# A half chunk of batch 0's queries loaded later, with buffers of its own, in a fused linear-attention and gated-MLP kernel

## The chip, the core and the metric

The kernel runs on one core of one Trainium2 chip. The metric is the device time of one execution in microseconds (us); for the kernel before, the median of 3 runs is 248.44 us (248.17 to 248.79). Times inside an execution are counted from its first instruction. TensorE is PE in the profile's rows (PEld is its weight load), VectorE is DVE, ScalarE is ACT, GpSimd is POOL, SyncE is SP.

## What is computed

Eight batches of eight heads, 576 positions and 64 columns go through a linear attention, and its result through a gated MLP. The reference, cut to what matters:

```python
theta = pi / 2 * pos / 576
phi(x) = concat([relu(x) * cos(theta), relu(x) * sin(theta)])   # 64 -> 128 columns
q_p, k_p = phi(q), phi(k)
kv  = einsum('bhsf,bhsd->bhfd', k_p, v)
z   = k_p.sum(over s)
out = (q_p @ kv) / (q_p @ z + 1e-6)      # per head; heads side by side: x, 4608 x 512
h   = ((x @ w1) * (x @ w2)) @ w3         # 512 -> 1024 -> 1024
y   = h @ w_out                          # 1024 -> 512, float32
```

## The kernel before

**Tiles.** A batch's 576 positions are five chunks: 0 to 3 of 128 rows and chunk 4, a half one, of 64. For each batch the queries, keys and values are loaded from DRAM by GpSimd's DMA queue and cast to bfloat16 on the way. Features (`features`, lines 487 to 499) are made chunk by chunk: the cosine half on VectorE (line 491), the sine half on ScalarE for the first `n` heads (line 495) and on VectorE for the rest (line 498). Values are copied into a buffer `va` that has a column of ones (`prep_v`, line 510), so that one product gives `kv` and `z`. `kv` (lines 534 to 544) takes 40 small matmuls (line 539), in the order of the chunks 4, 0, 1, 2, 3 for odd batches, and brings the sums from PSUM to `kvs`: heads 0 to 3 by ScalarE (543), then heads 4 to 7 by VectorE (544). A query chunk is transposed on TensorE and copied out of PSUM (`q_tr`, lines 553 to 563) or, in later batches, transposed by a DMA of SyncE's queue. `num` (565 to 573) multiplies it with `kvs` in 8 matmuls into a pair of PSUM banks `pnum`; `norm` (575 to 586) divides by the last column in three VectorE instructions (582, 583, 584). The quotient is transposed to `xT` (`x_tr`, 606 to 612; later by DMA, `x_dma`).

**The MLP.** Nine tiles of 512 rows of `x` go through `ffn_groups` (649 to 724): products with `w1` and `w2` (line 655), their elementwise product (681, 698), and the product with `w34 = w3 @ w_out` (703), all through a ring of four PSUM banks `ffnps` that `ffn_tile` hands out. `w34` is built once in the kernel (`w34_mm`, line 470): eight products of 8 matmuls on blocks of `w3` that VectorE has transposed (`w3_tr`, line 460, ring of 3 buffers), each evicted by ScalarE (line 473).

**What sets the order.** Every engine works in order, and the order is written out in the string `PLAN` (lines 26 to 259). In it `f t` is the next piece of MLP tile t (four matmuls of 512 columns mostly), `w j l n` a piece of the `w34` product, `t3 j` a transpose of `w3`, `l b q 0` a load (first 64 partitions; `1` is the second 64), `lg` and `lt` loads behind a gate on GpSimd, `q04` the load of batch 0's chunk 4 (line 419), `q b c n`, `k b c n` and `v b c E` the features and the value copy on engine E (G is GpSimd, V VectorE, A ScalarE), `qt b c E` a query transpose and its copy, `kv`, `n`, `d` and `xt` (or `xd` and `qd` by DMA) as above. An entry's place sets only the order on each engine's queue; whoever is free goes ahead.

**Around the change.** Batch 0's first 512 rows open the kernel. Its chunk 4 is needed only for the second MLP tile (`f 1`), so it is loaded with batch 1, while `w34` is built. The feature buffer `qp` is one for all batches: chunk 4 of batch 0 must have been transposed before batch 1's chunk 4 is written. `kv 1` needs all of batch 1's keys and values. GpSimd's DMA issues pass through eight semaphores in turn, so each issue waits for the landing of the eighth before it.

Of the kernel before, what the change touches and what calls it, by code (L numbers as in the profile page):

```python
# [106 lines left out]
f 2
f 2; d 3 4; k 4 2; q 4 1 0
f 2; xd 2 3; xd 3 0; k 4 1; k 4 0; xd 3 4; qd 4 3; n 3 2
f 2; n 3 3; l 5 v 0  # L110
f 2
f 2; q 4 2; d 3 2
f 2
f 2
f 2; qd 4 0
f 3; l 5 v 1; k 4 4
# [41 lines left out]
f 4; xd 4 4; xd 5 0; lt 7 v 0
# [1 line left out]
f 4; q 6 4  # L160
f 4; k 6 0 2; q 6 2; n 5 3; k 6 1 6; xd 5 4; q 6 0 4
f 4
# [10 lines left out]
f 5; kv 6; sg; k 7 3 6; lt 7 q 1; qd 6 2
f 5; n 5 2; k 7 2; k 7 1; k 7 0 4; lg 7 v 1; qd 6 0
f 5; qd 6 4; xd 5 3; qd 6 3
f 5
f 5; d 5 2; xd 5 1; xd 5 2
f 5
f 5; n 6 0; d 6 0; v 7 2 A; q 6 1 4; v 7 0 V
f 5; q 7 2; q 7 0  # L180
f 5; xd 6 0
# [130 lines left out]
def kernel(  # L312
# [128 lines left out]
    nc.vector.memset(oneb[:], 1.0)
# [42 lines left out]
                      "qpT": qpT_bufs[b % 2], "x": {}, "n": {}}  # L484
        return att[b]

    def features(dst, rows, c, at, n=H, cos=True, sin=True):

        R = ROWS[c]
        if cos:  # L490
            nc.vector.tensor_scalar(out=dst[:R, c, :, 0:D], in0=rows[:R], scalar1=0.0,  # L491
                                    scalar2=cosv[:R, at:at + 1], op0=ALU.max, op1=ALU.mult)
        if sin:
            if n > 0:
                nc.scalar.activation(out=dst[:R, c, 0:n, D:F], in_=rows[:R, 0:n], func=ACTF.Relu,  # L495
                                     scale=sinv[:R, at:at + 1], bias=0.0)
            if n < H:
                nc.vector.tensor_scalar(out=dst[:R, c, n:H, D:F], in0=rows[:R, n:H], scalar1=0.0,
                                        scalar2=sinv[:R, at:at + 1], op0=ALU.max, op1=ALU.mult)
# [52 lines left out]

    def q_tr(b, c, on):
        R = ROWS[c]
        pst = ps_tr.tile([P, 8, 128], BF16, name="pst")
        for h in range(H):
            nc.tensor.transpose(pst[:, h, :], att[b]["qp"][:, c, h, :], identb[:])
        cols = ds(columns_of(b, c), R)
        if on == "both":
            nc.scalar.copy(out=att[b]["qpT"][:, 0:4, cols], in_=pst[:, 0:4, 0:R])  # L560
            nc.vector.tensor_copy(out=att[b]["qpT"][:, 4:8, cols], in_=pst[:, 4:8, 0:R])
        else:
            on(out=att[b]["qpT"][:, :, cols], in_=pst[:, :, 0:R])

    def num(b, c, tile=None, heads=range(H)):
        rows = out_rows(b, c)
        at = columns_of(b, c) - rows.start
        qpT, kvs = att[b]["qpT"], att[b]["kvs"]
        nt = tile or pnum()
        for h in heads:  # L570
            nc.tensor.matmul(nt[:, h // 4, ds((h % 4) * 65, 65)], lhsT=qpT[:, h, ds(at, 128)],  # L571
                             rhs=kvs[:, h, :], start=True, stop=True)
        att[b]["n"][c] = nt

    def norm(b, c, g0=0, ng=2):
        rows, R = out_rows(b, c), ROWS[c]
# [5 lines left out]
        nc.vector.tensor_scalar_add(out=den[rows, 0:ng], in0=n4[:, :, :, 64], scalar1=1e-6)  # L582
# [1 line left out]
        nc.vector.tensor_tensor(out=xblk[rows, g0:g0 + ng], in0=n4[:, :, :, 0:D],  # L584
                                in1=den[rows, 0:ng].unsqueeze(3).to_broadcast([R, ng, 4, D]),
                                op=ALU.mult)
# [260 lines left out]
```

## Time and profile before

| what | us |
|---|---|
| median of 3 runs | 248.44 |
| the profiled execution's own time | 247.68 |
| its span, first to last instruction | 245.8 |
| TensorE busy | 238.9 |
| VectorE busy | 147.9 |
| ScalarE busy | 118.5 |
| GpSimd busy | 88.9 |

How to read it: the span is 1.88 us shorter than the execution's own time; what lies around it is the launch. Busy time is the sum of the instructions' own durations. A row of the timeline gives the start, the time from the first start to the last end of a merged run of like instructions, the engine, the line, the operation with its output and input, the count, and, in square brackets, how long the engine sat idle before it and on whom it waited. Matmuls are pipelined, so a row's duration runs past the start of the next row; the distance between two starts is what a row occupies. The granted TensorE clock was 1.00 throughout.

### The profile page before, as it was taken

The numbers are of one execution on the slowest core, as the hardware profiler recorded it, in microseconds if no ns is written. First come the engines' busy times: TensorE is split into PE (matmuls) and PEld (weight loads), VectorE is DVE, ScalarE is ACT, GpSimd is POOL, SyncE is SP. The second block draws the span as 40 slices with busy tenths as digits, with TensorE's granted clock in tenths as the row PEclk, the third lists the DMA queues.
The fourth block names the chain that finished last, engine by engine and source line by source line (L and its number), as shares of the span: only waits on it lengthen the run. The fifth ranks groups of instructions, "written<-read, shape, count | busy, mean of one in ns | idle before, by whom it ended". The sixth has DMA issues, their size and how long they took to land.

```text
span 245.8 us, 5011 instructions
## 1 busy us (share of the span) xinstructions
PE 238.9 (97%) x1891; PEld 129.9 (53%) x1891; DVE 147.9 (60%) x373; ACT 118.5 (48%) x210; POOL 88.9 (36%) x171
## 2 busy tenths in 40 slices
PE   8899999989999999999999999999999999999994
PEld 3589434567964545445544544454545454444442
DVE  6976558968888546925855576378458327403320
ACT  2834323767756734755466436558343333323321
POOL 8854887534403170006124023024001000497800
PEclk9999999999999999999999999999999999999999
DMA  7999999999999999879999999999337332489933
GB/s 198 195 196 199 195 177 191 199 199 168 165 163 167 182 135 195 129 138 153 193 138 148 168 144 159 234 148 185 75 61 148 96 75 44 68 267 338 302 119 128
DMA packets 84552, 40.44 MB, mean 165 GB/s; under 512 B 48048, under 2 KB 82096, under 8 KB 84528
## 3 DMA queue, kind: packets, MB, share of 16 engines
q0 software_dynamic: 38832, 27.27, 69.3%
q1 hardware_dynamic: 45696, 12.85, 32.6%
q8 instruction: 15, 0.25, 0.4%
q14 instruction: 9, 0.07, 0.1%
HBM read 38.80 MB, written 9.44 MB: 196 GB/s over the span
## 4 chain that ended last, share of the span: by engine, by line
PE 77%; DMA 9%; POOL 6%; DVE 4%; issue 1%; DVEq 0%; POOLq 0%
PE ffnps L655 45%; PE ffnps L703 24%; DMA early<-in_moe_w_out_dram 4%; PE pnum L571 4%; PE pnum L539 3%; POOL early L403 3%; DMA kf<-in_k_dram 3%; DMA q<-in_q_dram 2%; DVE w3T L460 1%; POOL w2b L776 1%; POOL early L409 1%; DVE kp L491 1%; POOL w1b L776 1%; PE ffnps L720 1%; DVE qp L491 1%
## 5 line engine op out<-in xcount | busy, mean ns | idle before, releaser
L698 DVE TENSOR_TENSOR abT<-asb,ffnps 128x512 bf16<-128x512 bf16 x64 | 43.7, 685 | 56.8 <-PE ffnps L655 56.4
L655 PE MATMUL ffnps<-xT,w1b 128*128 128x512 bf16 (+2 forms) x352 | 76.0, 340 | 0.0
L655 PE MATMUL ffnps<-xT,w2b 128*128 128x512 bf16 (+2 forms) x352 | 76.0, 340 | 0.0
L693 ACT CAST asb<-ffnps 128x512 bf16<-128x512 f32 x64 | 37.4, 584 | 58.6 <-PE ffnps L655 45.5
L703 PE MATMUL ffnps<-w34b,abT 128*128 128x512 bf16 x280 | 65.0, 379 | 0.0
L655 PEld LDWEIGHTS <-w1b 128*128 128x128 bf16 x352 | 31.7, 98 | 28.4
L655 PEld LDWEIGHTS <-w2b 128*128 128x128 bf16 x352 | 31.6, 98 | 28.0
L703 PEld LDWEIGHTS <-abT 128*128 128x128 bf16 x280 | 26.2, 98 | 28.9
L584 DVE TENSOR_TENSOR xblk<-pnum,den 128x512 bf16<-128x512 f32 (+1 forms) x39 | 26.9, 691 | 1.5 <-DVE den L583 0.2
L415 POOL COPY seen<-asb 128x1 bf16<-128x1 bf16 x13 | 2.6, 198 | 50.5 <-ACT asb L693 50.4
L495 ACT ACTIVATE kp<-kf,sinv 128x512 bf16<-128x512 bf16 (+4 forms) x33 | 20.7, 656 | 0.3 <-DMA kf<-in_k_dram 0.3
L495 ACT ACTIVATE qp<-qs,sinv 128x512 bf16<-128x512 bf16 (+6 forms) x30 | 18.3, 626 | 1.9 <-DMA qs<-in_q_dram 0.8
L571 PEld LDWEIGHTS <-qpT 128*128 128x128 bf16 x320 | 15.0, 98 | 7.2
L709 ACT COPY early<-ffnps 128x512 f32<-128x512 f32 x19 | 11.1, 585 | 15.4 <-PE ffnps L703 14.2
L571 PE MATMUL pnum<-kvs,qpT 128*128 128x65 bf16 x312 | 15.9, 194 | 0.0
L491 DVE TENSOR_SCALAR kp<-kf,cosv 128x512 bf16<-128x512 bf16 (+1 forms) x40 | 14.4, 379 | 2.1 <-DMA kf<-in_k_dram 2.1
L470 PE MATMUL ffnps<-early,w3T 128*128 128x512 bf16 x64 | 14.5, 379 | 0.5 <-DVE w3T L460 0.5
L415 POOL COPY seen<-xT 128x1 bf16<-128x1 bf16 x6 | 1.2, 193 | 36.6 <-DMA xT<-xblk 36.6
L510 POOL COPY va<-vs 128x512 bf16<-128x512 bf16 (+1 forms) x13 | 8.2, 639 | 13.7 <-DMA vs<-in_v_dram 13.7
L491 DVE TENSOR_SCALAR qp<-qs,cosv 128x512 bf16<-128x512 bf16 (+1 forms) x35 | 12.5, 368 | 0.0
L372 POOL DMA_DIRECT2D vs<-in_v_dram x16 | 10.7, 681 | 2.4 <-PE ffnps L470 1.1
L460 DVE STREAM_TRANSPOSE w3T<-early 128x1024 bf16<-128x1024 bf16 x8 | 9.7, 1231 | 2.5 <-DMA early<-in_moe_w_dram 2.5
(90 smaller groups left out, 225.5 us busy)
## 6 DMA issues: line engine op xcount, KB each, us to landing
kf<-in_k_dram POOLq DMA_DIRECT2D x7, 320.0 KB, 7.5
early<-in_moe_w_dram POOLq DMA_DIRECT2D x16, 128.0 KB, 5.3
out_dram<-osb POOLq DMA_DIRECT2D x8, 256.0 KB, 5.2
qs<-in_q_dram POOLq DMA_DIRECT2D x6, 320.0 KB, 6.6
vs<-in_v_dram POOLq DMA_DIRECT2D x6, 320.0 KB, 8.0
kf<-in_k_dram POOLq DMA_DIRECT2D x7, 256.0 KB, 8.2
qs<-in_q_dram POOLq DMA_DIRECT2D x6, 256.0 KB, 7.9
vs<-in_v_dram POOLq DMA_DIRECT2D x6, 256.0 KB, 9.3
```

The lines of the kernel that those rows point to most:

```text
L372: eng.dma_start(out=t[ts(half, 64), :, 0:j, :].rearrange("p h j d -> p h (j d)"), in_=rows[:, span, :].rearrange("h (p j) d -> p h (j d)", ...
L460: nc.vector.transpose(out=w3Ts[jp][:, l0:l0 + n, :].rearrange("p l (c i) -> p l c i", c=4), in_=w3b[:, jp, :].rearrange("p (c l j) -> p l ...
L470: nc.tensor.matmul(acc[:, :], lhsT=w3T[:, lc, :], rhs=woutb[:, lc, :], start=(lc == 0), stop=(lc == 7))
L491: nc.vector.tensor_scalar(out=dst[:R, c, :, 0:D], in0=rows[:R], scalar1=0.0, scalar2=cosv[:R, at:at + 1], op0=ALU.max, op1=ALU.mult)
L495: nc.scalar.activation(out=dst[:R, c, 0:n, D:F], in_=rows[:R, 0:n], func=ACTF.Relu, scale=sinv[:R, at:at + 1], bias=0.0)
L571: nc.tensor.matmul(nt[:, h // 4, ds((h % 4) * 65, 65)], lhsT=qpT[:, h, ds(at, 128)], rhs=kvs[:, h, :], start=True, stop=True)
L584: nc.vector.tensor_tensor(out=xblk[rows, g0:g0 + ng], in0=n4[:, :, :, 0:D], in1=den[rows, 0:ng].unsqueeze(3).to_broadcast([R, ng, 4, D]), ...
L655: nc.tensor.matmul(out, lhsT=w[:, kc, ts(jc, 128)], rhs=x[:, kc, tok], start=(kc == 0), stop=(kc == 3))
L693: nc.scalar.copy(out=asb[:], in_=aT[:, :])
L698: nc.vector.tensor_mul(out=abT[:, jc, :], in0=asb[:], in1=bT[:, :])
L703: nc.tensor.matmul(ops[:, :], lhsT=abT[:, jc, ts(ms, 128)], rhs=w34b[:, jc, :], start=(jc == 0), stop=(jc == 7))
L709: nc.scalar.copy(out=osb[:, ms % 2, :], in_=ops[:, :])
```

## The change

Four edits, made together with a new order in `PLAN` from the `w34` stage on.

1. The load `q04` moves from ahead of batch 1's loads to behind the last of them (`l 1 v 1`).
2. Its features go to a buffer of their own, `late`, laid over the first two heads of the raw queries of batch 0 (`q0f`), whose upper 64 rows are cleared with batch 1's value rows. Its features, transpose, numerator and quotient move from the middle of the `w34` stage to behind `kv 1`'s place on VectorE, TensorE and ScalarE.
3. Its numerator goes to two banks of the MLP's ring instead of the pair `pnum`, and is normalized in two halves.
4. Of batch 1's value copies, chunks 4, 0 and 1 on GpSimd and 3 and 2 on VectorE become chunk 0 on GpSimd, 1 on ScalarE, and 4, 2 and 3 on VectorE. GpSimd's one copy stands ahead of the load `l 2 v 1` in its queue.

The plan between, before and after, cut to the entries between the last loads of batch 1 and `f 1`:

```diff
-... w3 3 6 2; q04; l 1 q 0; l 1 q 1; l 1 k 0
+... w3 3 6 2; l 1 q 0; l 1 q 1; l 1 k 0
...
-f 0; xt 0 3 V; l 1 v 1
+f 0; xt 0 3 V; l 1 v 1; q04
...
-f 0
+f 0; v 1 0 G
...
-w 3 0 4
-w 3 4 4; t3 5; q 0 4 0; t3 6
+w 3 0 4; t3 5
+w 3 4 4; t3 6
 w 4 0 4
-w 4 4 4
-w 5 0 4; qt 0 4 V; t3 7; q 1 4 2; q 1 1; q 1 0 0
-w 5 4 4; n 0 4; q 1 3 0; d 0 4
+w 4 4 4; t3 7; q 1 4 2; q 1 2 0
+w 5 0 4
+w 5 4 4; q 1 1; q 1 0
 w 6 0 4
-w 6 4 4; q 1 2 4; k 1 4 0; k 1 0; l 2 v 1; v 1 4 G
-w 7 0 4; v 1 0 G; v 1 1 G; k 1 3 0; k 1 2
-w 7 4 4; k 1 1 0
-f 0; qt 1 4 A; qt 1 2 A; l 3 q 0; v 2 2 G; v 1 3 V
-f 0; qt 1 0 A; v 1 2 V; kv 1
-f 0; qt 1 1 A; n 1 4; d 1 4; k 2 4; k 2 2 2
+w 6 4 4; q 1 3 2; qt 1 4 A; v 1 4 V; k 1 4 4; qt 1 1 A; l 2 v 1
+w 7 0 4; k 1 0
+w 7 4 4; k 1 2 2; k 1 1 0; v 1 2 V; qt 1 0 A; l 3 q 0; k 1 3 0; v 1 1 A; v 1 3 V; v 2 2 G
 f 0
-f 0; n 1 0; d 1 0; xt 1 4 A; q 2 0 0; q 2 1; lt 3 v 0; xt 0 4 A
-f 0; v 2 0 G
-f 0; xt 1 0 V; n 1 1
-f 0
-f 1
+f 0; q 0 4 6; kv 1
+f 0; n 1 4; d 1 4; qt 0 4 A
+f 0; n 0 4; d 0 4; xt 1 4 A
+f 0; n 1 0; d 1 0
+f 0; xt 0 4 A
+f 0; q 2 0 4; q 2 1 2; n 1 1; v 2 0 G; xt 1 0 A; qt 1 2 A; lt 3 v 0
+f 1; qd 2 0; d 1 1; qd 2 1
...
```

From there to the end the entries of batches 2 to 7 are shuffled among the same pieces of the MLP: the same work on TensorE, some feature heads and value copies moved between VectorE and ScalarE, some DMA transposes in another order. The code beside the plan:

```diff
+    late = q0f[:, 0:2].rearrange("p h c d -> p (h c d)").bitcast(BF16).rearrange("p (h f) -> p h f", h=H)
...
+        else:
+            nc.vector.memset(late[64:128], 0.0)
...
     def prep_q(b, c, n=H, **kw):
         rows = raw[b, "q"][:, :, c, :] if b > 0 else q0f[:, :, c, :] if c < 4 else q04[:]
+        if (b, c) == (0, 4):
+            return features(late.unsqueeze(1), rows, c, NCH + c, n, at_chunk=0, **kw)
...
     def num(b, c, tile=None, heads=range(H)):
-        nt = tile or pnum()
+        if (b, c) == (0, 4):
+            nt = [ffn_tile(), ffn_tile()]
+            banks = [t[:, :] for t in nt]
+        else:
+            nt = tile or pnum()
+            banks = [nt[:, g, :] for g in range(2)]
...
     def norm(b, c, g0=0, ng=2):
+        nt = att[b]["n"][c]
+        if isinstance(nt, list):
+            if ng == 2:
+                norm(b, c, 0, 1)
+                return norm(b, c, 1, 1)
+            nt, at = nt[g0].unsqueeze(1), 0
...
```

More of the change, by code (lines that the diff above doesn't have):

```diff
@@ L93 @@
 f 2; lg 4 q 0
-f 2
-f 2; l 4 q 1; qd 3 1
-f 2
-f 2; lt 4 v 1; n 3 0; qd 3 4
-f 2
-f 2; qd 3 2
+f 2; lt 4 v 1; qd 3 0; qd 3 4
+f 2; l 4 q 1; qd 3 2
+f 2
+f 2; qd 3 3
+f 2; n 3 0
+f 2
 f 2
@@ L102 @@
 f 2; d 3 0
-f 2; xd 2 4; n 3 1
-f 2; q 4 0; q 4 4; d 3 1
-f 2; q 4 3; v 4 4 V; l 4 k 1; xd 3 1; n 3 4
-f 2
[L107 to L116, printed above, removed]
-f 3
-f 3; d 3 3; v 4 0 G; qd 4 2
-f 3; lg 5 k 0; v 5 2 V; lt 5 k 1; v 4 1 G
+f 2
+f 2; n 3 1; d 3 1; xd 3 0
+f 2; q 4 3
+f 2; n 3 4; q 4 4
+f 2; q 4 0; q 4 1 0; xd 3 1
+f 2; xd 2 3; l 4 k 1
+f 2; xd 2 4; k 4 2; d 3 4; v 4 4 V; xd 3 4; qd 4 3; k 4 1
+f 2; n 3 2
+f 2; k 4 0
+f 2; l 5 v 0
+f 2; q 4 2; n 3 3
+f 2; d 3 2
+f 2; qd 4 0; l 5 v 1
+f 3; k 4 4
+f 3
+f 3; v 4 0 G; qd 4 2
+f 3; lg 5 k 0; v 5 2 V; d 3 3; lt 5 k 1; v 4 1 G
 f 3
-f 3; k 4 3
+f 3; k 4 3 4; lg 5 q 0
 f 3
-f 3; v 4 2 A; lg 5 q 0; lt 5 q 1; v 4 3 V
+f 3; v 4 2 A; lt 5 q 1; v 4 3 V
 f 3; kv 4; v 5 0 V; lg 6 v 0; qd 4 1
@@ L157 @@
 f 4
[L158 removed]
+f 4; xd 5 0; lt 7 v 0
 f 4; v 6 2 A
[L160 to L162 removed]
+f 4; q 6 4; k 6 0 2; q 6 2; n 5 3; k 6 1 6; xd 5 4
+f 4; q 6 0 4
 f 5
@@ L165 @@
 f 5
-f 5
-f 5
-f 5; v 6 3 V
-f 5; d 5 1; k 6 2 0
-f 5; l 7 q 0; st
-f 5
-f 5
[L173 to L181, printed above, removed]
+f 5; k 6 2 0
+f 5
+f 5; v 6 3 V
+f 5; d 5 1
+f 5; l 7 q 0; kv 6; st
+f 5
+f 5
+f 5; sg; k 7 3 6; qd 6 2
+f 5; n 5 2; k 7 0 4; lt 7 q 1; k 7 2; k 7 1; lg 7 v 1; qd 6 0
+f 5; qd 6 4; xd 5 3; qd 6 3; xd 5 1
+f 5; d 5 2
+f 5; xd 5 2
+f 5
+f 5; n 6 0; d 6 0; q 6 1 4; v 7 2 G; v 7 0 V
+f 5; q 7 2; q 7 0 6; xd 6 0
+f 5
 f 5; q 7 4 2
 f 5; n 6 4
-f 5; d 6 4; xd 6 4
+f 5; d 6 4; st; xd 6 4
 f 5
-f 5; n 6 2; n 6 3; q 7 3 2
+f 5; n 6 2; n 6 3; q 7 3 4
 f 5
 f 6; v 7 3 V
-f 6; qd 6 1; d 6 2
-f 6; st; xd 6 2; gx 0
 f 6
+f 6; qd 6 1; d 6 2; q 7 1 6
 f 6; k 7 4
 f 6
-f 6; n 6 1
-f 6; d 6 1
+f 6
+f 6; n 6 1; d 6 1
 f 6; qd 7 2
-f 6; d 6 3; qd 7 4; v 7 4 V; q 7 1
-f 6; v 7 1 V
+f 6; gx 0; v 7 1 V; d 6 3; qd 7 4; xd 6 2
+f 6; v 7 4 V
+f 6
 f 6
@@ L485, in att_of, with features @@
         return att[b]
-    def features(dst, rows, c, at, n=H, cos=True, sin=True):
+    def features(dst, rows, c, at, n=H, cos=True, sin=True, at_chunk=None):
         R = ROWS[c]
+        c = c if at_chunk is None else at_chunk
         if cos:
@@ L554, in q_tr @@
         R = ROWS[c]
+        rows = late if (b, c) == (0, 4) else att[b]["qp"][:, c]
         pst = ps_tr.tile([P, 8, 128], BF16, name="pst")
         for h in range(H):
-            nc.tensor.transpose(pst[:, h, :], att[b]["qp"][:, c, h, :], identb[:])
+            nc.tensor.transpose(pst[:, h, :], rows[:, h, :], identb[:])
         cols = ds(columns_of(b, c), R)
@@ L568, in num @@
         qpT, kvs = att[b]["qpT"], att[b]["kvs"]
-        nt = tile or pnum()
+        if (b, c) == (0, 4):
[4 more added lines that the diff above has]
+            banks = [nt[:, g, :] for g in range(2)]
         for h in heads:
-            nc.tensor.matmul(nt[:, h // 4, ds((h % 4) * 65, 65)], lhsT=qpT[:, h, ds(at, 128)],
+            nc.tensor.matmul(banks[h // 4][:, ds((h % 4) * 65, 65)], lhsT=qpT[:, h, ds(at, 128)],
                              rhs=kvs[:, h, :], start=True, stop=True)
@@ L576, in norm @@
         rows, R = out_rows(b, c), ROWS[c]
-        n4 = att[b]["n"][c][rows, g0:g0 + ng, 0:260].rearrange("p g (h e) -> p g h e", e=65)
+        nt = att[b]["n"][c]
[4 more added lines that the diff above has]
+            nt, at = nt[g0].unsqueeze(1), 0
+        else:
+            at = g0
+        n4 = nt[rows, at:at + ng, 0:260].rearrange("p g (h e) -> p g h e", e=65)
         if g0 == 0:
```

68 lines of the change are left out of this document (35 added, 33 removed).

## The prediction

> **What bounds the kernel now.** I read the page's busy times first, then the busy time by stretches, then TensorE's timeline across the stage that the diff touches.
>
> ```profile
> PE 238.9 (97%) x1891; PEld 129.9 (53%) x1891; DVE 147.9 (60%) x373; ACT 118.5 (48%) x210; POOL 88.9 (36%) x171
> ```
> ```profile
> 30.00:40.00 10.00, 9.45 (x44) 4.06 (x43) 7.42 (x8) 2.73 (x5) 9.04 (x15) 1.00 1.42 180
> 40.00:50.00 10.00, 10.00 (x78) 5.57 (x76) 8.99 (x23) 6.64 (x13) 5.76 (x10) 1.00 1.39 198
> 50.00:60.00 10.00, 9.36 (x126) 6.19 (x124) 7.39 (x23) 6.44 (x14) 3.02 (x6) 1.00 1.36 196
> 60.00:246.00 186.00, 182.16 (x1343) 95.38 (x1340) 103.00 (x262) 89.37 (x162) 50.49 (x103) 1.00 0.93 155
> ```
>
> The second number of a row is TensorE's busy time. From 60 us on it is busy until it ends near 242 (182.16 us): no wait is left there to remove. In the stretch of the diff it is idle 0.55 us before 40 and 0.64 us after 50. VectorE is at 8.99 of 10 between 40 and 50.
>
> ```profile
> 35.94 6.22 PE L470 MATMUL ffnps<-early,w3T 128*128 128x512 bf16 x28 [0.55 <-DVE w3T L460]
> 49.64 0.61 PE L557 MATMUL pst<-identb,qp 128*128 128x128 bf16 x8
> 50.08 0.67 PE L539 MATMUL pnum<-va,kp 128*128 128x65 bf16 x16
> 51.27 1.23 PE L539 MATMUL pnum<-va,kp 128*128 128x65 bf16 x24 [0.52 <-DVE kp L498]
> 52.34 1.02 PE L703 MATMUL ffnps<-w34b,abT 128*128 128x512 bf16 x4
> 53.20 0.61 PE L557 MATMUL pst<-identb,qp 128*128 128x128 bf16 x8
> 53.65 0.42 PE L571 MATMUL pnum<-kvs,qpT 128*128 128x65 bf16 x8
> 53.91 1.89 PE L703 MATMUL ffnps<-w34b,abT 128*128 128x512 bf16 x8
> 55.63 0.42 PE L571 MATMUL pnum<-kvs,qpT 128*128 128x65 bf16 x8
> 55.99 0.30 PE L611 MATMUL pst<-identb,xblk 64*128 64x64 bf16 x8
> ```
>
> From start to start, four 512-column matmuls take 0.86 us (52.34 to 53.20), eight transposes 0.44 (49.64 to 50.08), eight 65-column matmuls 0.26 (53.65 to 53.91). So `kv 1`, 40 of the last kind, would take 1.30 and end at 51.38; it ends at 52.34. That is 0.96 lost, and 0.10 more at 55.63 (0.36 for 0.26): **1.06 us in all is what the edit can win at most.** The 0.55 at 35.94 is a wait for `w3`, loaded ahead of everything that moves; it stays.
>
> **Why `kv 1` is late**: VectorE's row.
>
> ```profile
> 36.38 3.52 DVE L460 STREAM_TRANSPOSE w3T<-early 128x1024 bf16<-128x1024 bf16 x3
> 40.89 0.35 DVE L491 TENSOR_SCALAR qp<-q,cosv 64x512 bf16<-64x512 bf16 x1 [1.00 <-DMA q<-in_q_dram]
> 44.51 0.30 DVE L498 TENSOR_SCALAR qp<-qs,sinv 64x384 bf16<-64x384 bf16 x1
> 44.74 0.60 DVE L491 TENSOR_SCALAR qp<-qs,cosv 128x512 bf16<-128x512 bf16 x2
> 45.26 0.34 DVE L498 TENSOR_SCALAR qp<-qs,sinv 128x512 bf16<-128x512 bf16 x1
> 47.76 0.28 DVE L498 TENSOR_SCALAR qp<-qs,sinv 128x256 bf16<-128x256 bf16 x1
> 47.96 0.34 DVE L491 TENSOR_SCALAR kp<-kf,cosv 64x512 bf16<-64x512 bf16 x1
> 49.64 1.31 DVE L491 TENSOR_SCALAR kp<-kf,cosv 128x512 bf16<-128x512 bf16 x2
> 51.14 0.64 DVE L510 COPY va<-vs 128x512 bf16<-128x512 bf16 x2
> 52.95 0.43 DVE L544 CAST kvs<-pnum 128x260 bf16<-128x260 f32 x1 [1.17 <-ACT kvs L543]
> ```
>
> VectorE waits 1.00 us for the half chunk (the only long wait), then works without a gap until the last value copy ends at 51.78. The change takes this wait away. What is late next?
>
> **Part by part.**
>
> *The load `q04` behind the values.*
>
> ```profile
> DMA packets 1056, 0.36 MB, mean 182 GB/s; under 512 B 550, under 2 KB 1055, under 8 KB 1055
> ```
> ```profile
> DMA packets 674, 0.40 MB, mean 200 GB/s; under 512 B 19, under 2 KB 674, under 8 KB 674
> ```
> ```profile
> 38.95 1.36 POOL L372 DMA_DIRECT2D vs<-in_v_dram  x2
> 48.08 0.70 POOL L510 COPY va<-vs 64x512 bf16<-64x512 bf16 x1 [0.71 <-DMA vs<-in_v_dram]
> 49.46 1.35 POOL L510 COPY va<-vs 128x512 bf16<-128x512 bf16 x2 [0.68 <-DMA vs<-in_v_dram]
> ```
>
> The first row is the DMA from 38 to 40 us, when the half chunk's 512 packets of 128 B pass; the second is 50 to 52 without them. 0.04 MB less in 2 us is 0.20 us lost, and its own 0.065 MB at 200 GB/s is 0.33: 0.53 us of queue. Bounds: 0.33 by bytes, 0.97 by packets (512 at 528 per us). Batch 1's loads, all behind it now, land that much sooner. The GpSimd rows give the landings of the values: first half by 48.08, second by 49.46. After: 47.55 and 48.93. GpSimd's issues keep their count, and each waits for the eighth before it as now; the values are issued at 38.95, 9 us ahead of their landing, so issuing sets nothing. `q04` lands about 49.5, and is used after 50.8 (below).
>
> *VectorE.* The transposes of `w3` go on at 39.90 without the wait, to 42.4. Then the query features that it has (chunks 4, 2, 1, 0, 3: five cosines at 0.26, two sines of six heads at 0.23, one of eight at 0.26) take 2.0 and end near 44.5. Then comes `v 1 4`, and it waits for the first half of the values: **VectorE stands still for some 3 us, with all of batch 1's key features queued behind it.** This is the added wait. From 47.55: the three value copies 0.32 each, five cosines 0.26, sines of 4, 6, 8 and 8 heads 0.20, 0.23, 0.26, 0.26: 3.21 us. GpSimd's single copy falls into it. In the row at 49.64, two cosines take 1.31 instead of 0.60 beside two GpSimd copies: 0.35 each; the bounds for one copy are 0 and 0.71, I take 0.35. End: 51.11.
>
> The Trainium skill, "SBUF — State Buffer", section "Who interferes with whom", says that VectorE and GpSimd take turns on a shared port pair under an exclusive lock, so that the later one stands still until the earlier one's whole instruction ends. The 1.31 agrees in direction, though 0.35 per instruction is less than a whole copy of 0.67; by the rule the copy would cost 0.67 and the sum below would be 0.32 higher.
>
> *ScalarE.*
>
> ```profile
> 43.51 0.72 ACT L495 ACTIVATE qp<-qs,sinv 128x512 bf16<-128x512 bf16 x1 [0.79 <-DMA qs<-in_q_dram]
> 44.14 0.57 ACT L473 CAST w34b<-ffnps 128x512 bf16<-128x512 f32 x1
> 45.97 0.51 ACT L495 ACTIVATE qp<-qs,sinv 128x256 bf16<-128x256 bf16 x1
> 48.53 1.50 ACT L563 COPY qpT<-pst 128x512 bf16<-128x512 bf16 x2 [0.23 <-PE pst L557]
> 49.91 0.60 ACT L709 COPY early<-ffnps 128x512 f32<-128x512 f32 x1
> 50.39 1.04 ACT L563 COPY qpT<-pst 128x1024 bf16<-128x1024 bf16 x1
> 52.54 0.38 ACT L543 CAST kvs<-pnum 128x260 bf16<-128x260 f32 x1 [1.10 <-PE pnum L539]
> 59.98 0.62 ACT L510 COPY va<-vs 128x512 bf16<-128x512 bf16 x1
> ```
>
> Starts give 0.63 for a sine of eight heads, 0.53 of four, some 0.3 of two, 0.48 for an eviction, 1.38 for one small and one large query copy (I split 0.46 and 0.92), 0.52 for a value copy. In its new order it has, from 43.1 (32 matmuls of 0.2165 after 35.94, and 0.2 to react): an eviction, two sines of eight, an eviction, two heads, the small copy, four heads, a large copy, eight heads, an eviction, two heads, a large copy, `v 1 1`: 7.3 us without a gap, to 50.4. Its cast of the last `w34` block ends near 48.6; TensorE needs it at 49.1. Then an eviction and `q 0 4` (0.55), and it is free near 51.4 for `kvs`. So it costs nothing, but with only 0.2 us to spare against VectorE: the second engine is close behind the first.
>
> *TensorE.* Ahead of `kv 1` it loses the half chunk's transposes (0.44) and numerator (0.26), and one large transpose trades places with another: `kv 1` can start at 50.08 − 0.70 = 49.38 and end at 50.68. It needs its last chunk's `v 1 3` from VectorE: 51.11 + 0.05 + 0.26 = 51.42. **Lost: 0.74 us.** (By ScalarE's `v 1 1`: 50.4 + 24 × 0.0325 = 51.2, not later.)
>
> *Behind `kv 1`.* `n 1 4` now follows after four matmuls (0.86) instead of four and a transpose (1.31). `kvs` is ready 1.04 us after the sums end (52.34 to 52.95 + 0.43): **0.2 us of new wait.** The half chunk's transpose and numerator then fill the time in which batch 1's first quotient is made (0.10 lost before, nothing after).
>
> ```profile
> 54.11 0.16 DVE L582 TENSOR_SCALAR den<-pnum 64x8 f32<-64x8 f32 x1 [0.73 <-PE pnum L571]
> 54.53 0.68 DVE L584 TENSOR_TENSOR xblk<-pnum,den 64x512 bf16<-64x512 f32 x1
> ```
>
> A quotient takes VectorE 1.10 us, 0.42 of it ahead of the product. The half chunk's, in two halves, takes twice 0.42 and some 0.8 for the products: 1.65, over which it holds two banks of the ring. TensorE meanwhile has two pieces, a small transpose and a numerator (2.2) before it needs the quotient, and the ring comes round later still. So it costs nothing; if VectorE is over 0.5 us late here, TensorE waits one to one.
>
> *From 60 us on* the same work in another order, under the cover that TensorE never waits there now: nothing, between 0 and one piece (0.86). The added clearing is one VectorE instruction in the first MLP tile, where TensorE's matmuls set the pace (VectorE waits for them): nothing.
>
> **Sum.** 1.06 lost before, 0.74 + 0.20 after: 0.12 us less. On the profiled execution 247.68 − 0.12 = 247.56; it stands 0.76 below the median of the runs shown, so 248.44 − 0.12 = **248.3**. A difference within 0.3% (0.74 us) can't be told from none.
>
> **Rivals.**
>
> 1. *The wait goes altogether.* The half chunk costs the queue 0.97, and the one GpSimd copy VectorE nothing: VectorE ends at 47.11 + 3.21 = 50.32, `kv 1` is dense, only the 0.2 is left: 247.6; with that hidden too 247.4. For it: packets, not bytes, seem to set the pace of small packets. Against: both ends must hold at once. 0.15.
> 2. *The other side: VectorE's head-of-line wait for `v 1 4`.* Should the values not land sooner (48.08), VectorE ends at 51.64 to 52.0, `kv 1` at 51.95 to 52.31: lost 1.27 to 1.63, plus 0.2: 0.4 to 0.8 more than before, 248.85 to 249.2, and 0.9 if the lock costs more. It decides from a landing of 47.7 on. For it: the 0.53 is a difference of two means, and all key features now hang on one landing. 0.22.
> 3. *The load's place doesn't matter*: it costs 0.33, ScalarE is the one that ends `kv 1`, and old and new losses are equal: 248.5. 0.13.
> 4. *A new wait in batches 2 to 7* where a shuffled feature or a transpose comes late: up to one piece, 249.0 to 249.3. Against: no TensorE wait there now. 0.1.
>
> The forecast itself (248.0 to 248.6) has 0.4. **How the numbers follow**: faster by over 0.3% is rival 1, 0.14; slower is half of rival 2 and most of 4, 0.2; within is the rest, 0.66. The range runs from rival 1's end, 247.4, to the upper ends of 2 and 4, 249.3.
>
> **What would show it.** In the profile after: no VectorE wait for the half chunk near 40; one of 2 to 3 us before a value copy, ending near 47.5; `kv 1` from 49.4 to 51.4 with its wait on VectorE; a small wait before the next numerator; no other. Wrong would be a first value copy at 48 or later, `kv 1` waiting on ScalarE, or a TensorE wait after 60 us.

## The result: about 0.4% slower

Over 22 executions each, the changed kernel's median is 249.2 us (248.17 to 251.35) and that of the kernel before 248.19 us (247.65 to 249.65): a ratio of 1.0037, 95% interval 1.002 to 1.0055. The forecast was 248.3, within a range of 247.4 to 249.3. The time lies at the range's upper end, and on the side to which the prediction gave a chance of 0.20. That it lies in the range at all is luck: the forecast counted from 248.44, and the kernel before came out 0.25 lower here. As a difference, −0.12 was forecast and the range ended at +0.86; measured were +1.01 by the medians and +0.92 by the ratio. The profiled execution took 249.28 us, with a span of 247.1.

First the page's busy times and the busy time by stretches, after the change (columns as before: stretch, length, busy us of TensorE, its weight loads, VectorE, ScalarE, GpSimd, granted clock, DMA share, GB/s).

```profile
PE 239.0 (97%) x1891; PEld 129.9 (53%) x1891; DVE 147.9 (60%) x384; ACT 119.3 (48%) x215; POOL 87.2 (35%) x167
```
```profile
30.00:40.00 10.00, 9.37 (x45) 4.01 (x43) 7.47 (x8) 2.64 (x5) 8.82 (x16) 1.00 1.38 185
40.00:50.00 10.00, 9.90 (x71) 5.33 (x70) 6.41 (x17) 8.12 (x16) 4.31 (x8) 1.00 1.44 196
50.00:60.00 10.00, 8.56 (x117) 5.62 (x117) 7.79 (x28) 5.31 (x13) 3.21 (x5) 1.00 1.31 186
60.00:249.00 189.00, 183.46 (x1355) 96.29 (x1351) 104.55 (x273) 89.85 (x164) 50.63 (x103) 1.00 0.94 153
```

The totals hardly moved. TensorE's busy time between 50 and 60 fell from 9.36 to 8.56, and VectorE's between 40 and 50 from 8.99 to 6.41. TensorE's timeline shows the place:

```profile
36.04 8.81 PE L473 MATMUL ffnps<-early,w3T 128*128 128x512 bf16 x40 [0.64 <-ACT w34b L476]
...
49.48 0.42 PE L545 MATMUL pnum<-va,kp 128*128 128x65 bf16 x8
51.38 1.18 PE L545 MATMUL pnum<-va,kp 128*128 128x65 bf16 x32 [1.48 <-POOL va L516]
52.39 1.02 PE L723 MATMUL ffnps<-w34b,abT 128*128 128x512 bf16 x4
53.48 0.42 PE L583 MATMUL pnum<-kvs,qpT 128*128 128x65 bf16 x8
...
55.04 0.42 PE L583 MATMUL ffnps<-kvs,qpT 128*128 128x65 bf16 x8
55.40 0.29 PE L631 MATMUL pst<-identb,xblk 64*128 64x64 bf16 x4
55.62 1.04 PE L723 MATMUL ffnps<-w34b,abT 128*128 128x512 bf16 x4
56.49 0.42 PE L583 MATMUL pnum<-kvs,qpT 128*128 128x65 bf16 x8
56.75 1.02 PE L723 MATMUL ffnps<-w34b,abT 128*128 128x512 bf16 x4
57.71 0.29 PE L631 MATMUL pst<-identb,xblk 64*128 64x64 bf16 x4
57.93 1.04 PE L723 MATMUL ffnps<-w34b,abT 128*128 128x512 bf16 x4
...
63.96 0.42 PE L583 MATMUL pnum<-kvs,qpT 128*128 128x65 bf16 x8
```

`kv 1` starts at 49.48, 0.60 earlier than before, does chunk 4's eight matmuls, and then stands 1.48 us for a value copy of GpSimd's. It ends at 52.39, where before it ended at 52.34. Without waits it would have taken 1.30, so 1.61 us are lost in it (0.96 before). The last row is batch 1's numerator of chunk 3; from there on the two kernels have the same work left. Before, it stood at

```profile
62.66 0.42 PE L571 MATMUL pnum<-kvs,qpT 128*128 128x65 bf16 x8
```

So all of the 1.30 us by which the two spans differ has arisen by then: 247.1 − 63.96 and 245.8 − 62.66 are both 183.14. VectorE, GpSimd and ScalarE after the change:

```profile
45.36 0.30 DVE L502 TENSOR_SCALAR qp<-qs,sinv 128x384 bf16<-128x384 bf16 x1
48.36 0.28 DVE L516 COPY va<-vs 64x512 bf16<-64x512 bf16 x1 [2.70 <-DMA vs<-in_v_dram]
...
49.78 0.34 DVE L495 TENSOR_SCALAR kp<-kf,cosv 128x512 bf16<-128x512 bf16 x1
50.05 0.34 DVE L502 TENSOR_SCALAR kp<-kf,sinv 128x512 bf16<-128x512 bf16 x1
50.31 0.28 DVE L516 COPY va<-vs 128x512 bf16<-128x512 bf16 x1
50.51 0.34 DVE L495 TENSOR_SCALAR kp<-kf,cosv 128x512 bf16<-128x512 bf16 x1
50.77 0.69 DVE L502 TENSOR_SCALAR kp<-kf,sinv 128x512 bf16<-128x512 bf16 x1
51.39 0.28 DVE L516 COPY va<-vs 128x512 bf16<-128x512 bf16 x1
...
54.35 0.68 DVE L604 TENSOR_TENSOR xblk<-pnum,den 64x512 bf16<-64x512 f32 x1
...
56.53 0.43 DVE L604 TENSOR_TENSOR xblk<-ffnps,den 64x256 bf16<-64x256 f32 x1
```
```profile
49.77 1.56 POOL L516 COPY va<-vs 128x512 bf16<-128x512 bf16 x1 [1.84 <-DMA vs<-in_v_dram]
```
```profile
49.78 0.63 ACT L516 COPY va<-vs 128x512 bf16<-128x512 bf16 x1
...
50.78 0.64 ACT L499 ACTIVATE q0f<-q,sinv 64x384 bf16<-64x384 bf16 x1
52.59 0.38 ACT L549 CAST kvs<-pnum 128x260 bf16<-128x260 f32 x1 [1.18 <-PE pnum L545]
```

VectorE stands 2.70 us at `v 1 4`, with the keys behind it, as the prediction has it. GpSimd's one copy, `v 1 0`, takes **1.56 us**; before, two of the same shape took 1.35 together. While it runs, VectorE passes four instructions at their usual spacing (49.78 to 50.77), and only the fifth is long, 0.69. So the copy seems to have stood behind VectorE for some 0.9 us, and then held VectorE up for about 0.35. `kv 1` needs that copy for its second chunk.

### The profile page after: what moved, and what is told of

Read it like the earlier page. It is cut to its first block, busy times and chain, and to the rows that moved or that the text cites. A ratio compares the mean times of both kernels' runs of the same rounds, so it can differ in the third digit from the quotient of the medians.

```text
span 247.1 us, 5028 instructions
## 1 busy us (share of the span) xinstructions
PE 239.0 (97%) x1891; PEld 129.9 (53%) x1891; DVE 147.9 (60%) x384; ACT 119.3 (48%) x215; POOL 87.2 (35%) x167
## 4 chain that ended last, share of the span: by engine, by line
PE 77%; DMA 12%; POOL 8%; issue 1%; DVE 0%; ACT 0%; POOLq 0%
PE ffnps L675 45%; PE ffnps L723 23%; DMA w2b<-in_moe_w_dram 5%; DMA vs<-in_v_dram 4%; PE pnum L583 4%; PE pnum L545 4%; POOL early L404 3%; DMA kf<-in_k_dram 3%; POOL kf L373 1%; POOL early L410 1%; PE ffnps L740 1%; POOL va L516 1%; POOL w2b L796 1%; POOL w1b L796 1%; POOL qs L373 1%
## 5 line engine op out<-in xcount | busy, mean ns | idle before, releaser
L718 DVE TENSOR_TENSOR abT<-asb,ffnps 128x512 bf16<-128x512 bf16 x64 | 43.8, 685 | 56.6 <-PE ffnps L675 52.3
L604 DVE TENSOR_TENSOR xblk<-pnum,den 128x512 bf16<-128x512 f32 (+1 forms) x38 | 26.2, 691 | 1.3
L499 ACT ACTIVATE kp<-kf,sinv 128x512 bf16<-128x512 bf16 (+5 forms) x34 | 20.8, 638 | 0.3 <-DMA kf<-in_k_dram 0.3
L495 DVE TENSOR_SCALAR kp<-kf,cosv 128x512 bf16<-128x512 bf16 (+1 forms) x40 | 13.9, 362 | 3.0 <-DMA kf<-in_k_dram 2.9
L495 DVE TENSOR_SCALAR qp<-qs,cosv 128x512 bf16<-128x512 bf16 (+1 forms) x35 | 11.9, 353 | 0.5 <-DMA qs<-in_q_dram 0.5
L729 ACT COPY osb<-ffnps 128x512 f32<-128x512 f32 x12 | 7.0, 585 | 10.1 <-PE ffnps L723 10.1
L545 PE MATMUL pnum<-va,kp 128*128 128x65 bf16 x280 | 10.2, 193 | 1.5 <-POOL va L516 1.5
L545 PEld LDWEIGHTS <-kp 128*128 128x128 bf16 x280 | 9.9, 97 | 3.2 <-issue 1.6
```

Of the source, the lines that this page charges most:

```text
L545: nc.tensor.matmul(kvt[:, h // 4, ds((h % 4) * 65, 65)], lhsT=a["kp"][:, c, h, :], rhs=a["va"][:, c, h, 0:D + 1], start=(i == 0 and h % 4 ...
L718: nc.vector.tensor_mul(out=abT[:, jc, :], in0=asb[:], in1=bT[:, :])
L729: nc.scalar.copy(out=osb[:, ms % 2, :], in_=ops[:, :])
```

## Three spans that add up

One way of cutting the stage held in every kernel that follows, and the experiments are read with it. **Landing** is when the second half of batch 1's values is there, as its first user sees it. The **tail** goes from there to the end of `kv 1` on TensorE. **Behind** goes from there to the numerator of chunk 3. Before: 49.46, a tail of 2.88 (to 52.34), 10.32 behind. After: 49.77, 2.62, 11.57. `kv 1` ends when the landing and the tail let it, however early TensorE is free; so TensorE work that moves from ahead of `kv 1` to behind it isn't hidden any more, it is added. The change moved the half chunk's transposes (0.44) and numerator (0.26) that way.

Theories: **P**, GpSimd's stretched copy beside VectorE's key features is what `kv 1` waits for. **L**, the values land no sooner, and VectorE's keys, queued behind the copy that waits for them, come too late. They separate where the copy goes and the keys' place stays, and the other way round.

## The experiments

The diffs show entries of the plan; ratios are to the kernel before, with 95% intervals.

**The GpSimd copy on ScalarE.**

```diff
-f 0; v 1 0 G
+f 0
-... l 3 q 0; k 1 3 0; v 1 1 A; v 1 3 V; v 2 2 G
+... l 3 q 0; k 1 3 0; v 1 0 A; v 1 1 A; v 1 3 V; v 2 2 G
```

> The changed kernel with batch 1's value copy of chunk 0 on ScalarE, ahead of that of chunk 1, instead of GpSimd. Theory P (shared port): in the changed kernel TensorE waits 1.48 us in kv 1 for GpSimd's copy, which took 1.56 us instead of 0.62 because VectorE's key features ran beside it. Without the copy VectorE is not disturbed either and ends at about 51.3 instead of 51.67; kv 1 ends at 51.6 instead of 52.39: 0.8 us less than the changed kernel, within 0.2 us of the kernel before. Theory L (landing): the values land no sooner than before and everything hangs on that; the copy only ends a little after VectorE, kv 1 ends at 52.0: 0.4 us less.

Ratio 0.9995 (0.9969 to 1.0021): no loss against the kernel before can be seen any more. TensorE's and GpSimd's timelines:

```profile
50.76 1.45 PE L545 MATMUL pnum<-va,kp 128*128 128x65 bf16 x32 [0.73 <-ACT va L516]
52.05 1.02 PE L723 MATMUL ffnps<-w34b,abT 128*128 128x512 bf16 x4
```
```profile
48.91 2.50 POOL L373 DMA_DIRECT2D vs<-in_v_dram  x1 [0.69 <-DMA vs<-in_v_dram]
```

The wait in the middle of `kv 1` halves, from 1.48 to 0.73. The first half of the values landed at 48.65 here, 0.29 later than after the change, and yet `kv 1` ends 0.34 earlier: 3.40 us from that landing to the end, against 4.03. So the copy costs 0.63 (the expectations had 0.8 by P and 0.4 by L). What is left is VectorE's late keys: its last copy ends at 51.70, 0.35 before `kv 1`. P is the larger part, and L what comes next. GpSimd's next instruction, which hands out a DMA, is now the one stretched beside VectorE's features: 2.50 instead of 0.68. Nothing waits for it soon.

**VectorE's keys ahead of its value copies**, with the GpSimd copy as it is.

```diff
-w 6 4 4; q 1 3 2; qt 1 4 A; v 1 4 V; k 1 4 4; qt 1 1 A; l 2 v 1
+w 6 4 4; q 1 3 2; qt 1 4 A; k 1 4 4; qt 1 1 A; l 2 v 1
-w 7 4 4; k 1 2 2; k 1 1 0; v 1 2 V; qt 1 0 A; l 3 q 0; k 1 3 0; v 1 1 A; v 1 3 V; v 2 2 G
+w 7 4 4; k 1 2 2; k 1 1 0; k 1 3 0; v 1 4 V; v 1 2 V; qt 1 0 A; l 3 q 0; v 1 1 A; v 1 3 V; v 2 2 G
```

> The changed kernel with VectorE's value copies of chunks 4 and 2 moved behind all key features of batch 1 (GpSimd's copy stays). Theory L, head of line: VectorE no longer stands still 2.7 us for the values with the keys behind it; keys are done by about 49.0, only copies of 0.2 us follow the landing at 49.8, and GpSimd's copy has no features beside it, 0.65 us, so kv 1 ends at 51.5: 0.9 us less than the changed kernel, level with before. Theory P alone (the copy is slow whatever VectorE does at the time, as on a bad execution): copy still 1.5 us, kv 1 ends at 52.4, no gain.

Ratio 0.9997 (0.9966 to 1.0028). GpSimd, VectorE and TensorE:

```profile
49.96 0.67 POOL L516 COPY va<-vs 128x512 bf16<-128x512 bf16 x1 [1.83 <-DMA vs<-in_v_dram]
```
```profile
48.92 0.28 DVE L516 COPY va<-vs 64x512 bf16<-64x512 bf16 x1
49.86 0.91 DVE L516 COPY va<-vs 128x512 bf16<-128x512 bf16 x2 [0.66 <-DMA vs<-in_v_dram]
```
```profile
50.68 1.18 PE L545 MATMUL pnum<-va,kp 128*128 128x65 bf16 x32 [0.61 <-POOL va L516]
51.69 1.02 PE L723 MATMUL ffnps<-w34b,abT 128*128 128x512 bf16 x4
```

VectorE's keys are done by 48.92, so the copy has no run of features beside it, and takes 0.67 again. VectorE's two copies beside it take 0.91 instead of the 0.48 that two take below. The tail falls from 2.62 to 1.83. The copy stays and its length goes: it is what VectorE does beside it that made it long.

**The load's old place** (`q04` back ahead of `l 1 q 0`, the rest as after the change).

```diff
-... w3 3 6 2; l 1 q 0; l 1 q 1; l 1 k 0
+... w3 3 6 2; q04; l 1 q 0; l 1 q 1; l 1 k 0
-f 0; xt 0 3 V; l 1 v 1; q04
+f 0; xt 0 3 V; l 1 v 1
```

> The changed kernel with only the load of the half query chunk put back ahead of batch 1's loads. If the load's place is worth what I put on it (0.53 us of queue), the values land 0.5 us later than in the changed kernel and it is 0.5 us slower than that, ratio to before about 1.006. Rival: the place is worth nothing that shows beside the scatter of the landings: the same as the changed kernel, ratio 1.004.

Ratio 1.0023 (0.9998 to 1.0049), landing 49.67, tail 2.63. This can't be told from the changed kernel's 1.0037. The copy is stretched here too, to 1.57.

**No such load at all**: the tile is filled by a memset, so batch 0's last 64 query rows are not computed from their data.

```diff
-    nc.gpsimd.dma_start(q04...)
+    nc.gpsimd.memset(q04[0:64], 1.0)
```

> The changed kernel without the load of the half query chunk (GpSimd fills its buffer with ones instead, so batch 0's last 64 rows of the output are wrong). As the load stands behind the values already, it should not bring them sooner: the same as the changed kernel within 0.2 us, values landing at 48.3 and 49.7. Rival: the load's 128-byte packets disturb the values beside them (16 DMA engines do not finish together), then the second half of the values lands 0.3 to 0.4 sooner and the time falls by as much.

Ratio 1.0024 (0.999 to 1.0059). GpSimd's row of this kernel:

```profile
49.21 1.55 POOL L516 COPY va<-vs 128x512 bf16<-128x512 bf16 x1 [3.22 <-DMA vs<-in_v_dram]
```

Even with the values there at 49.21, the copy takes 1.55 and the tail is 2.62. The loss in `kv 1` is 1.59: the landing moves the whole stage and takes nothing from the wait inside it. An earlier landing alone would not have been enough. Nor do the load's packets, when it stands behind the values, hold these up: from the landing of the first half of batch 1's queries to that of the second half of its values it is 7.25 us here and 7.24 after the change.

**After's copies in the kernel before**, everything else as before.

```diff
-v 1 4 G
+v 1 4 V
-w 7 0 4; v 1 0 G; v 1 1 G; k 1 3 0; k 1 2
+w 7 0 4; v 1 0 G; k 1 3 0; k 1 2
-f 0; qt 1 0 A; v 1 2 V; kv 1
+f 0; v 1 1 A; qt 1 0 A; v 1 2 V; kv 1
```

> The kernel before with only the value copies of the change: chunk 0 on GpSimd, 1 on ScalarE, 4, 2 and 3 on VectorE (the half query chunk stays first). Theory P: GpSimd's copy starts at about 49.5, beside VectorE's key features, and takes 1.5 us again; kv 1's chunk 0 waits until 51.0, kv 1 ends at 52.1 (52.34 in the kernel before): the same within 0.3 us. Rival: the copy takes 0.65 to 0.7 as the copies in the kernel before did, kv 1 ends at 51.7 and the kernel is 0.6 us faster than before.

Ratio 0.9995 (0.9973 to 1.0017): no difference. GpSimd and TensorE:

```profile
49.81 1.64 POOL L510 COPY va<-vs 128x512 bf16<-128x512 bf16 x1 [2.11 <-DMA vs<-in_v_dram]
```
```profile
51.50 1.18 PE L539 MATMUL pnum<-va,kp 128*128 128x65 bf16 x32 [0.86 <-POOL va L510]
```

```profile
50.49 0.48 DVE L510 COPY va<-vs 128x512 bf16<-128x512 bf16 x2
```

The stretched copy is here too, and `kv 1` waits for it. VectorE is free of the contention and done with its copies at 50.97 (51.78 before), but the tail is still 2.71, against 2.88. Taking copies off GpSimd only moved the price from VectorE to the copy that was left. (After 64 us, TensorE waited 3.5 us for a DMA transpose in this profiled execution; the median of the timed runs, 248.21, has no sign of it, so only rows up to 64 us are read.)

**Before's copies in the changed kernel.**

```diff
-f 0; v 1 0 G
+f 0
-w 6 4 4; q 1 3 2; qt 1 4 A; v 1 4 V; k 1 4 4; qt 1 1 A; l 2 v 1
+w 6 4 4; q 1 3 2; qt 1 4 A; k 1 4 4; qt 1 1 A; l 2 v 1; v 1 4 G
-w 7 0 4; k 1 0
+w 7 0 4; k 1 0; v 1 0 G; v 1 1 G
-... k 1 1 0; v 1 2 V; qt 1 0 A; l 3 q 0; k 1 3 0; v 1 1 A; v 1 3 V; v 2 2 G
+... k 1 1 0; qt 1 0 A; l 3 q 0; k 1 3 0; v 1 3 V; v 1 2 V; v 2 2 G
```

> The changed kernel with the value copies as before: chunks 4, 0 and 1 on GpSimd, 3 and 2 on VectorE. VectorE no longer stands still for the values and is through with the key features by 49. Theory P: GpSimd's copies of chunks 0 and 1 then take 0.65 each, the second ends at 51.2, kv 1 at 52.3: as the changed kernel, 0.8 us slower than before. Theory L (head of line is the whole loss): with VectorE free again kv 1 ends at 51.5, level with before.

Ratio 1.0032 (1.0008 to 1.0057): slower than before, and not to be told from the changed kernel. GpSimd and VectorE:

```profile
49.13 1.72 POOL L516 COPY va<-vs 64x512 bf16<-64x512 bf16 x3
```
```profile
49.60 1.61 DVE L516 COPY va<-vs 128x512 bf16<-128x512 bf16 x2 [0.95 <-DMA vs<-in_v_dram]
```

VectorE's keys were done early, and GpSimd's three copies take 0.57 each. This time it is VectorE's two copies that are stretched, 1.61 instead of the 0.48 that two took in the kernel above. The same contention, with the other loser; the tail is 2.17. `kv 1` ends at 51.77, between the 52.3 of P and the 51.5 of L. So P in its narrow form (the one copy on GpSimd) is not the whole of it: VectorE's copies can be the ones that stand. By this execution some 0.5 us of the loss should be back; the timed ratio, with its interval, neither shows that nor rules it out.

**All five copies on VectorE**, behind the keys.

```diff
-f 0; v 1 0 G
+f 0
-... qt 1 4 A; v 1 4 V; k 1 4 4; qt 1 1 A; l 2 v 1
+... qt 1 4 A; k 1 4 4; qt 1 1 A; l 2 v 1
-w 7 4 4; k 1 2 2; k 1 1 0; v 1 2 V; qt 1 0 A; l 3 q 0; k 1 3 0; v 1 1 A; v 1 3 V; v 2 2 G
+w 7 4 4; k 1 2 2; k 1 1 0; k 1 3 0; v 1 4 V; v 1 0 V; v 1 1 V; v 1 2 V; qt 1 0 A; l 3 q 0; v 1 3 V; v 2 2 G
```

> The changed kernel with all of batch 1's value copies on VectorE, behind its key features, and none on GpSimd or ScalarE. Copies of 0.2 us each from the landing at 49.8: chunk 3 is there at 50.7, kv 1 ends at 51.0 instead of 52.39. 1.3 us less than the changed kernel, 0.2 less than before (the new waits behind kv 1, 0.6 us in sum, stay). If the values land later than 50, all shifts with them.

Ratio 0.9984 (0.9955 to 1.0013). VectorE and TensorE:

```profile
49.40 0.90 DVE L516 COPY va<-vs 128x512 bf16<-128x512 bf16 x4 [0.68 <-DMA vs<-in_v_dram]
```
```profile
49.74 1.18 PE L545 MATMUL pnum<-va,kp 128*128 128x65 bf16 x32 [0.29 <-DVE va L516]
50.76 1.02 PE L723 MATMUL ffnps<-w34b,abT 128*128 128x512 bf16 x4
```

One engine copies four chunks in 0.90 us, less than the 1.56 that GpSimd took for one. The tail is 1.36, and the loss in `kv 1` 0.43.

**The half chunk's transposes ahead of batch 1's first numerator**, on top of that.

```diff
-f 0; n 1 4; d 1 4; qt 0 4 A
+f 0; qt 0 4 A; n 1 4; d 1 4
```

> As all_vector, and the half chunk's transposes stand ahead of batch 1's first numerator, so that TensorE has 0.44 us of work while kvs is copied. If the 0.23 us that TensorE waited before that numerator is the wait for kvs, it goes: 0.2 us less than all_vector. Rival: ScalarE's copy of the transposes then comes ahead of something else, or the time moves to the next wait: the same as all_vector.

Ratio 0.997 (0.9951 to 0.999): faster than before. TensorE:

```profile
51.49 0.61 PE L564 MATMUL pst<-identb,q0f 128*128 128x128 bf16 x8
51.94 0.42 PE L583 MATMUL pnum<-kvs,qpT 128*128 128x65 bf16 x8
...
53.06 0.42 PE L583 MATMUL ffnps<-kvs,qpT 128*128 128x65 bf16 x8
53.56 0.29 PE L631 MATMUL pst<-identb,xblk 64*128 64x64 bf16 x4
...
62.12 0.42 PE L583 MATMUL pnum<-kvs,qpT 128*128 128x65 bf16 x8
```

The transposes cover the 0.23 of waiting for `kvs`. TensorE then stands 0.24 (0.50 from 53.06 to 53.56, where the numerator takes 0.26) ahead of batch 1's small transposes, whose quotient is ready only at 53.50, so that the span behind falls only from 11.57 to 11.49.

**The load's old place once more**, on top of that.

```diff
-... w3 3 6 2; l 1 q 0; l 1 q 1; l 1 k 0
+... w3 3 6 2; q04; l 1 q 0; l 1 q 1; l 1 k 0
-f 0; xt 0 3 V; l 1 v 1; q04
+f 0; xt 0 3 V; l 1 v 1
```

> all_vector_swap with the load of the half chunk ahead of batch 1's loads again. In all_vector_swap kv 1 follows the landing of the values by 0.2 us steps and TensorE is dense through it, so a later landing shows at once. If the place of the load is worth its 0.4 us of queue, the values land at 49.7 instead of 49.27, kv 1 loses some 0.3 us and the ratio to before is about 0.9985 instead of 0.997. Rival: the place is worth nothing: 0.997, and values at 49.3.

Ratio 0.9985 (0.9964 to 1.0005), landing 49.95 (as VectorE sees it), tail 1.36. Again the interval overlaps that of the same kernel with the load behind (0.997).

**Both halves' last transposes together**, on top of the kernel with the swap.

```diff
-f 0; n 0 4; d 0 4; xt 1 4 A
+f 0; n 0 4; d 0 4
-f 0; xt 0 4 A
+f 0; xt 1 4 A; xt 0 4 A
```

> all_vector_swap with the transposes of the two half chunks (batch 1's and batch 0's) side by side again, as in the kernel before, instead of one piece of the MLP apart. In all_vector_swap TensorE waits 0.24 us for the first of them, and each takes 0.22 us from start to start where the two together took 0.23: side by side both prices go, 0.3 to 0.45 us less, ratio 0.9955. Rival: TensorE then waits as long for the second quotient, and nothing is won: 0.997.

Ratio 0.9958 (0.9935 to 0.9981), median 247.26 beside 248.11: **faster than both kernels.** TensorE:

```profile
49.17 1.53 PE L545 MATMUL pnum<-va,kp 128*128 128x65 bf16 x40
...
55.30 0.30 PE L631 MATMUL pst<-identb,xblk 64*128 64x64 bf16 x8
...
61.56 0.42 PE L583 MATMUL pnum<-kvs,qpT 128*128 128x65 bf16 x8
```

`kv 1` runs without a gap, the eight small transposes are one run again, and the numerator of chunk 3 comes 1.10 us sooner than before. The gain, 0.42% or some 1.0 us, is about the size of what the prediction named as the most that the edit could win (1.06).

**All in one table** (us; the landing as GpSimd sees it, with 0.10 added where VectorE saw it first, which is the difference in the one kernel where both waited, 49.96 and 49.86). "Worked out" is the tail plus the span behind, less the 13.20 of before, plus a landing of −0.15 where the load is behind the values, 0 where it is ahead and −0.54 without it; the landings are one execution each, so these are means: 49.75 for the four kernels with the load ahead, 49.60 for six with it behind, and the one landing of 49.21 without.

| kernel | landing | tail | behind | worked out | timed |
|---|---|---|---|---|---|
| before | 49.46 | 2.88 | 10.32 | | |
| after | 49.77 | 2.62 | 11.57 | +0.34% | +0.37% |
| load ahead | 49.67 | 2.63 | 11.57 | +0.40% | +0.23% |
| no load | 49.21 | 2.62 | 11.56 | +0.18% | +0.24% |
| copy on ScalarE | 50.06* | 1.99 | 11.56 | +0.08% | −0.05% |
| keys first | 49.96 | 1.73 | 11.57 | −0.02% | −0.03% |
| before's copies | 49.70 | 2.07 | 11.57 | +0.12% | +0.32% |
| after's copies in before | 49.81 | 2.71 | 10.32 | −0.07% | −0.05% |
| all on VectorE | 49.50 | 1.26 | 11.57 | −0.21% | −0.16% |
| with the swap | 49.37 | 1.26 | 11.49 | −0.24% | −0.30% |
| swap, load ahead | 50.05 | 1.26 | 11.49 | −0.18% | −0.15% |
| swap, joined | 49.27 | 1.27 | 11.02 | −0.43% | −0.42% |

(* nobody waited for the second half here; 1.41 added to the first, as after the change. By the landings that the traces keep it came 0.33 after that of the changed kernel, 49.98 against 49.65, which would make it 50.10. In the last two a record is missing at the end of `kv 1`, and it is counted back from the next piece.) Every worked-out figure lies inside its timed interval.

So the cause: the change adds 1.25 us behind `kv 1` and gives back 0.26 in the tail and perhaps 0.15 in the landing. Of the 1.25, 0.70 is work moved there, 0.23 a wait for `kvs`, 0.21 comes of the half chunks' eight small transposes, which are two runs of four now, each about as long as the one of eight, and 0.10 is a second pause ahead of such a run (1.24 together). The pause is no wait for the quotient: TensorE stands 0.10 ahead of the runs at 55.40 and 57.71, and VectorE has written their quotients by 55.03 and 56.96 (the rows at 54.35 and 56.53). What it waits for, no view shows. The tail had 1.62 to give (2.88 to 1.26). GpSimd's copy beside VectorE's features, and the keys queued behind a copy that waits, kept most of it: taking away the copy, or the features beside it, brings the time back to that of before. What stays open is what the load's place is worth: the two pairs of kernels that differ in nothing else point in opposite directions (1.0023 and 1.0037, 0.9985 and 0.997), within their intervals, and none of the timed differences below 0.3% can be told from none by itself.

## Why the prediction was wrong, step by step

- *What bounds the kernel* was right: the stage around `kv 1`, nothing from 60 us on, and 0.96 of the 1.06 to win; the other 0.10 is no wait for data (below).
- *The load behind the values* **failed.** "Batch 1's loads, all behind it now, land that much sooner": 0.53, so 47.55 and 48.93. The trace has 48.36 and 49.77, 0.84 late for the second; by the means of the table, 0.15 was won of the 0.53. The load itself did move. The DMA after the change, in the two stretches of 38 to 40 and 48 to 50:

```profile
DMA packets 720, 0.39 MB, mean 197 GB/s; under 512 B 36, under 2 KB 719, under 8 KB 719
```
```profile
DMA packets 1015, 0.38 MB, mean 192 GB/s; under 512 B 494, under 2 KB 1014, under 8 KB 1014
```

  Its small packets are gone from 38 to 40 (36 now, 550 before) and pass at 48 to 50. But landings differ by 0.59 among four kernels with the load ahead (49.46 to 50.05) and by 0.69 among six with it behind: a single landing of a full queue doesn't carry a term of 0.5. The one of before, from which the sum started, was the earliest of its four. The landings that the traces keep show where the term fails. From the first half of batch 1's queries to the second half of its values it is 7.20 to 7.32 us in all twelve traces, with the load ahead, behind or gone. What differs is when those queries land. From the last block of `w3` to them it is 2.17 to 2.70 us with the load between, 1.66 to 2.51 with it behind, and 2.36 with no load: batch 1's loads used the room that the load left only in part, if at all (0.11 by the means, 2.32 and 2.21). Why, no run here shows. A first value copy at 48 or later was among the signs of being wrong that the prediction named.
- *VectorE* was right in kind: a stop of 2.70 at `v 1 4` (some 3 expected), and 0.35 lost beside the copy (0.62 from 50.77 to 51.39, where 0.26 is usual). From landing to its last copy it took 3.31 (3.56 expected).
- "*GpSimd's single copy falls into it* … the bounds for one copy are 0 and 0.71, I take 0.35" **failed**: the sum looked for the price of contention on VectorE only. In the trace of before the copies came through in 0.70 and 0.67 and VectorE stood; nothing there showed the opposite case. The copy's own 0.9 us were in no term, and it is the copy that `kv 1` waited for, 0.41 after VectorE would have let it end (51.67 + 0.31 = 51.98; it ended at 52.39). VectorE was 0.25 quicker than reckoned, and by this luck the tail was wrong by only 0.13 (2.49 expected).
- By the Trainium skill's rule that the prediction weighed ("SBUF — State Buffer", "Who interferes with whom"), an engine that finds the pair taken stands until the other's instruction has ended, and whichever issued first wins. The runs agree that either side can lose: VectorE's copies in two kernels (1.61 and 0.91 for two), GpSimd's in four. On how long, the rule read as a stand of one instruction is too short: the copy took some 0.9 us more than usual, while four VectorE instructions passed in a row. That it stood all this time and then ran is a reading of these rows; no view shows it waiting.
- *ScalarE* was right: `v 1 1` ended at 50.41 (50.4 expected), and it then waited 1.18 for the sums.
- *Behind `kv 1`*: 0.2 for `kvs` was right (0.23). That the half chunk "costs nothing" **failed**: four small transposes take 0.22 (55.40 to 55.62, and again from 57.71) where eight took 0.23, and TensorE pauses 0.10 ahead of each four. The working had read the one such pause of before, at 55.63, as a wait for a quotient, and as won. But that quotient was written by 55.21 (54.53 + 0.68), and its transposes start at 55.99; the pause stayed and came twice. By its terms the span behind would have grown by 0.80 (0.70 + 0.20 − 0.10); it grew by 1.25.
- *The sum*: by the means, 0.38 too much for the landing, 0.13 too little for the tail and 0.45 too little behind. −0.12 with these is +0.84, the worked-out figure of the table (0.34%; 0.37% timed).
- *After 60 us* was right: TensorE has no wait there, and rival 4 falls. Rival 1 didn't come; rival 3 falls, since ScalarE ended nothing.
- *Rival 2* names the condition that came true (a landing after 47.7) and a range, 248.85 to 249.2, that ends where the median lies, but with VectorE as the last engine. It was GpSimd. As a difference it gave 0.4 to 0.8 more than before, or 0.9 with a dearer lock, and 0.92 was measured. With its condition resting on a difference of two means against such scatter, it deserved more than 0.22.

## What to carry to other kernels

When a stage's end hangs on a transfer, count from the landing: work taken from ahead of it is not won, and work put behind it is paid in full. Let an in-order engine do what is there already before it does what waits for data, and let one engine make the copies that are due together: VectorE made four in 0.90 us, while beside another engine one took up to 1.64. And when two engines contend, price both as the loser, each with the consumer that waits for it.

## What had not been expected of the hardware

- A 128 x 512 copy from SBUF to SBUF on GpSimd took 1.55 to 1.64 us in four kernels where VectorE ran key features without a pause beside it, and 0.61 to 0.74 in those where VectorE had none or stood. What decides who stands isn't settled: in the kernel before, also beside key features, GpSimd's copies came through (1.35 for two) and two VectorE cosines took 1.31.
- A DMA issue of GpSimd's was stretched likewise, from 0.68 to 2.50 us, beside the same run on VectorE; one trace shows it.
- The landing of the same loads scatters by 0.6 to 0.7 us over traces of one execution each. The scatter is there when batch 1's first queries land (41.84 to 42.69 us); from then on all twelve traces need 7.20 to 7.32 us. Where it comes from before that, no run here shows.
